# Which tiles of x are turned by DMA, and how k and q of batches 3 to 7 reach their slots

## The chip, the cores and the metric

The kernel runs on one core of one Trainium2 chip. Its time is the device time of one execution in microseconds (us). All figures of the kernel before come from three timed runs and from one execution that was taken with the hardware profiler.

## The reference

The first stage is linear attention with a norm in each head, the second a layer norm, two matmuls with a ReLU between them and a residual:

```python
# q, k, v: (8 batches, 8 heads, 576 rows, 64), float32
kv  = einsum('bhsd,bhse->bhde', k, v)
out = einsum('bhsd,bhde->bhse', q, kv)
out = out / sqrt(mean(out*out, -1) + 1e-6) * g_norm
x   = out.transpose(0, 2, 1, 3).reshape(8, 576, 512)

xn  = (x - mean(x)) / sqrt(var(x) + 1e-6) * g_ln
y   = x + maximum(xn @ w_ch1, 0) @ w_ch2     # w_ch1: 512 x 2048, w_ch2: 2048 x 512
```

## The kernel before, in words

The 8 x 576 = 4608 rows are cut into 36 tiles of 128 rows. A batch has 512 rows in four full tiles, and its last 64 rows share a tile with those of its neighbour: tiles 0 to 3 are batch 0, 4 to 7 batch 1, tile 8 the rests of both; 9 to 12 are batch 2, 13 to 16 batch 3, tile 17 their rests; and so on, so that batches 4, 5, 6 and 7 begin with tiles 18, 22, 27 and 31. Four tiles make a block of the second stage; there are nine blocks. Blocks 0 and 1 do their first matmul tile by tile (`m1_fine`, L582), the others for four tiles at once (`m1_block`, L597, 16 groups of four matmuls of 128x512). The second matmul (`m2`, L616) goes tile by tile in four groups of four. ScalarE evicts each group of the first matmul with a ReLU (L589, L604), VectorE adds the residual to the second (`y_out`, L623), and a DMA from SyncE's queue stores the tile (L629). The matmuls' PSUM tag "mm" has four banks, so TensorE may be at most four groups ahead of the evictions.

Ahead of that lies the work for each batch. GpSimd's queue (POOL) loads k, q and v and turns float32 into bfloat16 on the way. kv is built on TensorE (`kv_mm`, L428) from `kp`, in which k stands in slots of 128 rows with all heads side by side. q stands likewise in `qp`, and one DMA transpose from SyncE's queue (`q_turn_dma`, L420, 128 x 2560 elements) makes `qT` of a whole batch from it. There are three ways for k and q into the slots. Batches 0 and 1 have their own. Batch 2 loads k into `kb` (L232) and q into `qb` (L239) as they lie in memory, 1 KB of four rows at a time, and ScalarE copies them into slot order (L380, two copies for each, 128x1024). Batches 3 to 7 load straight into `kp` and `qp` (`load_slots`, L260, 256 bytes at a time), with no copy. The last 64 rows of each batch come in by a small load of their own (L247).

For each tile the chain is: attention output on TensorE (`t_out`, L451), square on ScalarE (L464), sums and products on VectorE (L473, L468), root on ScalarE (L477), reciprocal, x, its mean (L482 to L520), and xc = (x - mean) * g_ln in bfloat16 (L525). xc must then be turned into `xT`, which the first matmul reads. Tiles 0 to 11 are turned on TensorE (`t_turn_pe`, L532, four transposes) and copied out of PSUM by ScalarE (`t_turn_out`, L539). Tiles 12 to 35 are turned by a DMA transpose from SyncE's queue (`t_turn_dma`, L543).

Nothing is ordered at run time: a planner inside the kernel gives each step a due time and a cost, plays the queues through and writes every engine's instructions down in the order that it finds. An engine works its own list strictly in that order and waits where data are not there. So an instruction that waits holds up everything behind it on its engine. This goes for SyncE too, whose list holds the stores, the turns of q and the turns of x in one row.

GpSimd's loads are held back by "gates": a copy of one element into `mark` (L690) that waits until a certain tile's `xT` is there, for instance tile 11's for k of batch 4, tile 12's for its q, tile 13's for its v. From batch 3 on a second mark (L694, `gate_turn`) holds each k load until the turn of q of the batch before has landed:

```python
            def gate_turn():
                if b >= 3:
                    pool_do(0.1, lambda: nc.gpsimd.tensor_copy(
                        mark, att[b - 1]["qT"][:, 0, 0:1]), [adone[b - 1]["qfree"]])
```

Of the kernel before, what the change touches and what calls it, by code (L numbers as in the profile page):

```python
# [14 lines left out]
def kernel(  # L15
# [11 lines left out]
    nc = tc.nc  # L27
# [6 lines left out]
    B, H, S, D = q.shape  # L34
# [8 lines left out]
    N_TILES = B * S // 128  # L43
    N_BLK = N_TILES // 4
    FINE = (0, 1)
    N_PE_TURN = 12
    N_SUM = 12
    LOOK = 8
    XB = 18
# [129 lines left out]
    def act_cost(n):  # L179
        return n / 1400 + 0.115, n / 1400 + 0.23  # L180
# [33 lines left out]
    kb = [consts.tile([128, H * 6 * D], bf16, name=f"kb{i}") for i in range(2)]  # L214
# [3 lines left out]
    kp = [consts.tile([128, 6, H, D], bf16, name=f"kp{i}") for i in range(2)]  # L218
    qp = [consts.tile([128, 5, H, D], bf16, name=f"qp{i}") for i in range(2)]
    mark = consts.tile([128, 1], bf16, name="mark")  # L220
# [7 lines left out]
    def load_kv(buf, src, b, h0=0, h1=H):  # L228
        t = 6 if b < 2 else 4
        n = 576 if b < 2 else 512  # L230
        def fn():
            nc.gpsimd.dma_start(  # L232
                kv_view(buf, b)[:, h0:h1, :, :].rearrange("p h t d -> p h (t d)"),
                src[b, h0:h1, 0:n, :].rearrange("h (p t) d -> p h (t d)", t=t))
        return fn, n * (h1 - h0) * 256

    def load_q(b, t0, t1):
        def fn():
            nc.gpsimd.dma_start(  # L239
                qb[:, :, t0:t1, :].rearrange("p h t d -> p h (t d)"),  # L240
                q[b, :, 0:512, :].rearrange("h (p t) d -> p h t d", t=4)[:, :, t0:t1, :]
                .rearrange("p h t d -> p h (t d)"))
        return fn, 128 * H * (t1 - t0) * 256
# [7 lines left out]
    def load_slot(dst, src, b, t, h0=0, h1=H):  # L251
# [2 lines left out]
                dst[:, t, h0:h1, :],  # L254
                src[b, h0:h1, 0:512, :].rearrange("h (p t) d -> p t h d", t=4)[:, t, :, :])
        return fn, 128 * (h1 - h0) * 256

    def load_slots(dst, src, b):
        def fn():
            nc.gpsimd.dma_start(  # L260
                dst[:, 0:4, :, :],
                src[b, :, 0:512, :].rearrange("h (p t) d -> p t h d", t=4))
        return fn, 128 * H * 4 * 256


    groups = []
# [24 lines left out]
    att = [dict() for _ in range(B)]  # L291
    done = [dict() for _ in range(N_TILES)]
    adone = [dict() for _ in range(B)]


    rate6, rate4, rate1 = 400.0, 395.0, 305.0
# [24 lines left out]
    def pool_load(name, fnb, rate=425.0, deps=()):  # L321
        fn, nb = fnb
        s = add_dma("POOL", 0, deps, fn, nb, rate)
        load.setdefault(name, []).append(s)
# [339 lines left out]
    def plan_batch(b):  # L664
        p = pos[FIRST[b]]
        ok = okey[FIRST[b]]
        kperm = []
        if b == 1:
            for h0, h1 in ((0, 4), (4, 8)):
                kperm.append(add("ACT", 1.2, 1.35, p - 18, load["k", 1],  # L670
                                 lambda h0=h0, h1=h1: k_permute(nc.scalar, 1, h0, h1)))
            for t in range(5):
                key = (p - 17 + 3 * t) if t < 4 else pos[8] - 40
                if t < 4:
                    qperm = add("ACT", *act_cost(512), key, load["q", 1],
                                lambda t=t: q_permute(nc.scalar, 1, t, t + 1))
                    qread = qperm
                else:
                    qperm = load["q", 1, 4][0]
                add_q_turn_pe(1, t, [qperm, z1[1]], key + 1, ("DVE", "ACT")[t % 2])  # L680
            vdeps = load["v", 1]
            adone[1]["qread"] = qread
            adone[1]["qfree"] = adone[1]["qT", 4][0]
        else:
            f = FIRST[b]
            def gate(n):

                if b >= 3:
                    m, i = divmod(n, 4)
                    pool_do(0.1, lambda: nc.gpsimd.tensor_copy(  # L690
                        mark, blk[m]["xT"][:, 0, i * 128:i * 128 + 1]), done[n]["xT"])
            def gate_turn():
                if b >= 3:
                    pool_do(0.1, lambda: nc.gpsimd.tensor_copy(  # L694
                        mark, att[b - 1]["qT"][:, 0, 0:1]), [adone[b - 1]["qfree"]])
            dk = [adone[b - 2]["kvmm"]]
            if b < 4:

                pool_do(0.5, lambda: nc.gpsimd.memset(kp[b % 2][no_fifth(b), 4, :, :], 0.0), dk)
            gate(f - 7 if b > 3 else 5)  # L700
            gate_turn()
            by_slot = b >= 3
            if by_slot:
                pool_load(("k", b), load_slots(kp[b % 2], k, b), rate1, dk)
            else:
                pool_load(("k", b), load_kv(kb, k, b), rate4, dk)
            pool_load(("k", b), load_fifth(kp[b % 2][:, 4, :, :], k, b), 180.0, dk)
            def some_q():
                gate(f - 6 if b > 3 else 6)
                if by_slot:  # L710
                    pool_load(("q", b), load_slots(qp[b % 2], q, b), rate1, [adone[b - 2]["qfree"]])
                else:
                    pool_load(("q", b), load_q(b, 0, 4), rate4, [adone[b - 1]["qread"]])
                pool_load(("q", b), load_fifth(qp[b % 2][:, 4, :, :], q, b), 180.0,
                          [adone[b - 2]["qfree"]])
            def some_v():
                gate(f - 5 if b > 3 else 7)
                pool_load(("v", b), load_kv(vb, v, b), rate4, dk)
                pool_load(("v", b), load_fifth(v5[b % 2], v, b), 100.0, dk)
            for load_some in (some_v, some_q) if b == 2 else (some_q, some_v):  # L720
                load_some()
            for h0, h1 in ((0, 4), (4, 8))[by_slot * 2:]:
                kperm.append(add("ACT", 0.85, 1.0, ok - 16, load["k", b][0:1] + dk,
                                 lambda h0=h0, h1=h1: k_permute(nc.scalar, b, h0, h1)))
            qperm = []
            for t0, t1 in ((0, 2), (2, 4))[by_slot * 2:]:
                qperm.append(add("ACT", 0.85, 1.0, ok - 14, load["q", b][0:1] + [
                    adone[b - 2]["qfree"]], lambda t0=t0, t1=t1: q_permute(nc.scalar, b, t0, t1)))
            for x in kperm + qperm:
                x.lag = 4.0 if b == 2 else 6.0  # L730
            kperm += load["k", b]
            turn = add_dma("SP", ok - 12, qperm + load["q", b] + (
                adone[b - 3].get("outs", []) if b >= 3 else []),
                           lambda: q_turn_dma(b), 2.6e3, 1.0, occ=2.98, lat=0.25, tail=0.42)
            for t in range(5):
                adone[b]["qT", t] = [turn]
            adone[b]["qfree"] = turn
            turn.lag = 5.0 if by_slot else 0.0
            adone[b]["qread"] = qperm[-1] if qperm else None
            vdeps = load["v", b]  # L740
        outs_before = adone[b - 3].get("outs", []) if b >= 3 else []
        s = add("PE", 1.12 if b > 1 else 1.34, 1.35 if b > 1 else 1.57, (p - 17.5 if b == 1 else ok - 4), vdeps + kperm,
                lambda: kv_mm(b, range(HP)), alloc="kvt")
        a = add("DVE", 0.34, 0.38, (p - 17 if b == 1 else ok - 2), [s, z1[4], z1[5]] + outs_before,
                lambda: kv_out(b, 0, HP, nc.vector, False))
        a2 = add("DVE", 0.34, 0.38, (p - 17 if b == 1 else ok - 2), [a], lambda: kv_out(b, 0, HP, nc.vector, True))
        s.frees = a2
        s.lag = 5.0 if b > 2 else 2.0 if b == 2 else 0.0
        adone[b]["kvmm"] = s
        adone[b]["kv"] = [a2]  # L750


    def plan_tile(n):
        bs, t = TILES[n]
        m, i = divmod(n, 4)
        p = pos[n]
# [38 lines left out]
        for h0, h1 in halves:  # L795
            ff = dict(f0=h0 * D, f1=h1 * D)
            w = (h1 - h0) / H
            xc = add("DVE", 0.6 * w + 0.06, 0.6 * w + 0.15, q0 + 8, [mean, load["gl"][0]],
                     lambda ff=ff: t_xc(n, **ff))
            if n < N_PE_TURN:  # L800
                tp = add("PE", 0.23 * w, 0.23 * w + 0.22, q0 + 9, [xc, ident, m1_before],
                         lambda ff=ff: t_turn_pe(n, **ff), alloc="kvt")
                tp.frees = add("ACT", *cost(act_cost, h0, h1), q0 + 10, [tp],
                               lambda ff=ff: t_turn_out(n, **ff))
                turned.append(tp.frees)
            else:
                turned.append(add_dma("SP", q0 + 9, [xc, m1_before], lambda: t_turn_dma(n),
                              0.5e3, 1.0, occ=1.235, lat=0.25, tail=0.42))
# [145 lines left out]
```

## Time and profile before

| | |
|---|---|
| median of 3 runs | 295.69 us (295.5 to 296.31) |
| the profiled execution's own time | 296.31 us |
| its span in the profile | 294.5 us |
| TensorE busy | 283.4 us, 96% of the span |
| VectorE / ScalarE / GpSimd busy | 165.7 / 143.1 / 66.1 us |
| DMA | 35.21 MB in 106652 packets, of which 85507 under 512 bytes |

The span is the time between the first and the last instruction of the profile; 1.81 us of the execution lie outside it. Engines are named PE (TensorE matmul), PEld (its weight loads), DVE (VectorE), ACT (ScalarE), POOL (GpSimd), SP (SyncE); a q behind the name is that engine's instruction queue. A line such as L597 is the line of the kernel before. "Landing" of a DMA is the time from its issue to its completion.

### The profile page before, as it was taken

The numbers are of one execution on the slowest core, as the hardware profiler recorded it, in microseconds if no ns is written. First come the engines' busy times: TensorE is split into PE (matmuls) and PEld (weight loads), VectorE is DVE, ScalarE is ACT, GpSimd is POOL, SyncE is SP. The second block draws the span as 40 slices with busy tenths as digits, with TensorE's granted clock in tenths as the row PEclk, the third lists the DMA queues.
The fourth block names the chain that finished last, engine by engine and source line by source line (L and its number), as shares of the span: only waits on it lengthen the run. The fifth ranks groups of instructions, "written<-read, shape, count | busy, mean of one in ns | idle before, by whom it ended". The sixth has DMA issues, their size and how long they took to land.

```text
span 294.5 us, 5143 instructions
## 1 busy us (share of the span) xinstructions
PE 283.4 (96%) x2045; PEld 161.2 (55%) x2045; DVE 165.7 (56%) x359; ACT 143.1 (49%) x288; POOL 66.1 (22%) x92
## 2 busy tenths in 40 slices
PE   3989999999999999999999989999999999999994
PEld 1989955977754445444544445444544444444443
DVE  1596048669777877557655764577557755320022
ACT  3278963978847612761276127611761176016400
POOL 8973220208007116120422208020000000000000
PEclk9999999999999999999999999999999999999999
DMA  7999999549989998997399799998201310220012
GB/s 98 186 200 205 204 198 194 162 91 124 185 183 78 120 167 164 175 121 181 64 124 100 94 210 120 123 148 164 56 18 56 89 53 18 67 95 1 0 73 72
DMA packets 106652, 35.21 MB, mean 120 GB/s; under 512 B 85507, under 2 KB 102147, under 8 KB 106628
## 3 DMA queue, kind: packets, MB, share of 16 engines
q0 software_dynamic: 72608, 18.35, 64.8%
q1 hardware_dynamic: 33860, 16.39, 23.5%
q8 instruction: 16, 0.26, 0.4%
q10 hardware_dynamic: 160, 0.13, 0.2%
q14 instruction: 8, 0.07, 0.1%
HBM read 36.70 MB, written 9.44 MB: 157 GB/s over the span
## 4 chain that ended last, share of the span: by engine, by line
PE 87%; DMA 7%; POOL 3%; DVE 1%; issue 1%; ACT 0%; ACTq 0%; POOLq 0%
PE mm_ps L616 39%; PE mm_ps L597 33%; PE mm_ps L582 8%; DMA w<-in_moe_w_ch_dram 5%; PE kv_ps L428 3%; PE out_ps L451 3%; DMA xT<-xc 3%; POOL qp L253 1%; POOL w L333 1%; PE xT_ps L532 1%; POOL kb L232 1%; POOL vb L232 0%; PE qT_ps L400 0%; DVE ss L473 0%; DVE x L503 0%
## 5 line engine op out<-in xcount | busy, mean ns | idle before, releaser
L616 PE MATMUL mm_ps<-w,m 128*128 128x512 bf16 (+1 forms) x592 | 130.2, 373 | 0.0
L597 PE MATMUL mm_ps<-xT,w 128*128 128x512 bf16 x448 | 100.8, 379 | 0.8 <-DMA xT<-xc 0.8
L604 ACT ACTIVATE m<-mm_ps 128x512 bf16<-128x512 f32 x112 | 66.8, 597 | 51.3 <-PE mm_ps L597 50.3
L616 PEld LDWEIGHTS <-m 128*128 128x128 bf16 x592 | 56.7, 98 | 59.8
L597 PEld LDWEIGHTS <-w 128*128 128x128 bf16 x448 | 43.0, 98 | 49.6 <-issue 1.2
L623 DVE SCALAR_TENSOR_TENSOR x<-mm_ps,rstd,x 128x512 f32<-128x512 f32 (+1 forms) x37 | 27.1, 734 | 42.2 <-PE mm_ps L616 42.1
L473 DVE TENSOR_REDUCE ss<-sq 128x8 f32<-128x512 f32 (+1 forms) x37 | 24.8, 670 | 46.2 <-ACT sq L464 46.1
L464 ACT ACTIVATE sq<-out_ps 128x512 f32<-128x512 f32 (+1 forms) x37 | 21.5, 584 | 50.8 <-PE out_ps L451 50.8
L582 PE MATMUL mm_ps<-xT,w 128*128 128x128 bf16 x512 | 30.9, 219 | 0.9 <-ACT xT L539 0.7
L582 PEld LDWEIGHTS <-w 128*128 128x128 bf16 x512 | 29.3, 98 | 1.9 <-issue 0.8
L525 DVE SCALAR_TENSOR_TENSOR xc<-x,mv,gl 128x512 bf16<-128x512 f32 (+1 forms) x37 | 27.1, 737 | 1.3 <-DVE mv L520 0.2
L468 DVE TENSOR_TENSOR xg<-out_ps,gn 128x512 f32<-128x512 f32 (+1 forms) x37 | 24.8, 669 | 0.2
L690 POOL COPY mark<-xT 128x1 bf16<-128x1 bf16 x15 | 5.5, 365 | 80.4 <-DMA xT<-xc 67.7
L589 ACT ACTIVATE m<-mm_ps 128x512 bf16<-128x512 f32 x32 | 18.3, 597 | 3.0 <-PE mm_ps L582 2.3
L503 DVE TENSOR_TENSOR x<-xg,inv 128x512 f32<-128x512 f32 x24 | 16.6, 692 | 0.8
L519 DVE BATCH_NORM_STATS2 stats<-x 128x6 f32<-128x512 f32 x24 | 16.6, 690 | 0.5
L477 ACT ACTIVATE rms<-ss,eps_attn 128x8 f32<-128x8 f32 (+1 forms) x37 | 11.0, 298 | 9.9 <-DVE ss L473 9.9
L451 PEld LDWEIGHTS <-qT 128*128 128x128 bf16 x160 | 11.5, 98 | 7.2 <-DVE kv_pack L443 0.3
L443 DVE CAST kv_pack<-kv_ps 64x256 bf16<-64x256 f32 (+1 forms) x18 | 7.1, 392 | 14.2 <-PE kv_ps L428 14.1
L451 PE MATMUL out_ps<-kv_pack,qT 128*128 128x128 bf16 x160 | 15.0, 220 | 0.1
L428 PE MATMUL kv_ps<-vb,kp 128*128 128x128 bf16 (+1 forms) x144 | 11.8, 234 | 3.0 <-DMA vb<-in_v_dram 3.0
L428 PEld LDWEIGHTS <-kp 128*128 128x128 bf16 (+1 forms) x168 | 11.1, 105 | 4.3 <-DVE kp L382 2.3
(61 smaller groups left out, 172.0 us busy)
## 6 DMA issues: line engine op xcount, KB each, us to landing
out_dram<-x SPq DMA_DIRECT2D x32, 256.0 KB, 2.8
w<-in_moe_w_ch_dram POOLq DMA_DIRECT2D x8, 512.0 KB, 12.6
vb<-in_v_dram POOLq DMA_DIRECT2D x6, 512.0 KB, 9.3
kp<-in_k_dram POOLq DMA_DIRECT2D x5, 512.0 KB, 8.2
qp<-in_q_dram POOLq DMA_DIRECT2D x5, 512.0 KB, 9.9
qb<-in_q_dram POOLq DMA_DIRECT2D x2, 512.0 KB, 15.8
out_dram<-x SPq DMA_DIRECT2D x6, 128.0 KB, 5.5
qp<-in_q_dram POOLq DMA_DIRECT2D x10, 64.0 KB, 8.5
```

The source lines that it names most:

```text
L428: nc.tensor.matmul(ps[:, hp, :], lhsT=kp[b % 2][p, t, 2 * hp:2 * hp + 2, :].rearrange("p h d -> p (h d)"), rhs=(v5[b % 2][:, 2 * hp:2 * hp ...
L451: nc.tensor.matmul(o3[:, hp, :], lhsT=att[b]["qT"][:, 4 * t + hp, :], rhs=kv_pack[b % 3][:, hp, :], start=(i == 0), stop=(i == len(bs) - 1))
L464: nc.scalar.activation(sq[:, h0:h1, :], st[n]["ps", h0][:, h0:h1, :], func=AF.Square)
L468: nc.vector.tensor_mul(xg[:, h0:h1, :], st[n]["ps", h0][:, h0:h1, :], gn.to_broadcast([128, h1 - h0, D]))
L473: nc.vector.tensor_reduce(ss[:, h0:h1, :], st[n]["sq"][:, h0:h1, :], axis=AX.X, op=ALU.add)
L525: nc.vector.scalar_tensor_tensor(xc[:, f0:f1], in0=st[n]["x"][:, f0:f1], scalar=blk[m]["mv"][:, i, 0:1], in1=gl[:, f0:f1], op0=ALU.subtrac ...
L582: nc.tensor.matmul(ps[:, d, :], lhsT=w1[c][:, kk, d * 128:(d + 1) * 128], rhs=blk[m]["xT"][:, kk, i * 128:(i + 1) * 128], start=(kk == 0), ...
L589: nc.scalar.activation(st[n]["m1"][:, c, :, :], st[n]["m1ps", c], func=AF.Relu)
L597: nc.tensor.matmul(ps, lhsT=w1[c][:, kk, d * 128:(d + 1) * 128], rhs=blk[m]["xT"][:, kk, :], start=(kk == 0), stop=(kk == nKm - 1))
L604: nc.scalar.activation(blk[m]["m1", c][:, d, :], blk[m]["m1ps", g], func=AF.Relu)
L616: nc.tensor.matmul(st[n]["m2ps", f0], lhsT=m1_piece(n, c, d), rhs=w2[c][:, d, f0:f1], start=(c == 0 and d == 0), stop=(c == 3 and d == 3))
L623: nc.vector.scalar_tensor_tensor(x[:, f0:f1], in0=st[n]["m2ps", f0], scalar=blk[m]["rstd"][:, i, :], in1=x[:, f0:f1], op0=ALU.mult, op1=AL ...
```

## The change

Two parts. First, the x of tiles 8, 9 and 10 is turned by DMA from SyncE's queue; tiles 0 to 7 and 11 stay on TensorE. Second, batches 3 to 7 go the way of batch 2: k and q are loaded as they lie into `kb` and `qb`, and ScalarE copies them into the slots, two copies of 128x1024 for k and two for q; the wait of a k load for the turn of q of the batch before stays for batch 3 alone. `qb` is one buffer, so a q load now waits for the q copies of the batch before. Together with the second part the planner is told other delays for the turn of q (`lag`), since it now comes behind copies.

```diff
-    N_PE_TURN = 12
+    PE_TURN = (0, 1, 2, 3, 4, 5, 6, 7, 11)
...
-    def load_slots(dst, src, b):
...
             def gate_turn():
-                if b >= 3:
+                if b == 3:
                     pool_do(0.1, lambda: nc.gpsimd.tensor_copy(
-                        mark, att[b - 1]["qT"][:, 0, 0:1]), [adone[b - 1]["qfree"]])
+                        mark, att[2]["qT"][:, 0, 0:1]), [adone[2]["qfree"]])
...
-            by_slot = b >= 3
-            if by_slot:
-                pool_load(("k", b), load_slots(kp[b % 2], k, b), rate1, dk)
-            else:
-                pool_load(("k", b), load_kv(kb, k, b), rate4, dk)
+            pool_load(("k", b), load_kv(kb, k, b), rate4, dk)
...
-                if by_slot:
-                    pool_load(("q", b), load_slots(qp[b % 2], q, b), rate1, [adone[b - 2]["qfree"]])
-                else:
-                    pool_load(("q", b), load_q(b, 0, 4), rate4, [adone[b - 1]["qread"]])
+                pool_load(("q", b), load_q(b, 0, 4), rate4, [adone[b - 1]["qread"]])
...
-            for h0, h1 in ((0, 4), (4, 8))[by_slot * 2:]:
+            for h0, h1 in ((0, 4), (4, 8)):
                 kperm.append(add("ACT", 0.85, 1.0, ok - 16, load["k", b][0:1] + dk,
                                  lambda h0=h0, h1=h1: k_permute(nc.scalar, b, h0, h1)))
             qperm = []
-            for t0, t1 in ((0, 2), (2, 4))[by_slot * 2:]:
+            for t0, t1 in ((0, 2), (2, 4)):
                 qperm.append(add("ACT", 0.85, 1.0, ok - 14, load["q", b][0:1] + [
                     adone[b - 2]["qfree"]], lambda t0=t0, t1=t1: q_permute(nc.scalar, b, t0, t1)))
...
-            turn.lag = 5.0 if by_slot else 0.0
-            adone[b]["qread"] = qperm[-1] if qperm else None
+            adone[b]["qread"] = qperm[-1]
...
-            if n < N_PE_TURN:
+            if n in PE_TURN:
```

What the planner makes of it can be read in the order of the two programs' instructions. On PE only the 12 transposes of tiles 8 to 10 go; every other instruction keeps its place. On SP the turns of tiles 8 and 9 stand behind the store of tile 4, that of tile 10 behind the store of tile 5, then come the store of tile 6 and the turn of q of batch 3; later the turn of tile 19 stands ahead of the turn of q of batch 5, behind which it stood before. On ACT three copies of `xT` go and 20 copies into slots come. On POOL four marks go.

More of the change, by code (lines that the diff above doesn't have):

```diff
@@ L256, in load_slot @@
         return fn, 128 * (h1 - h0) * 256
-    def load_slots(dst, src, b):
[L259 to L263, printed above, removed]
     groups = []
```

## The prediction

> **What bounds the kernel now.** I read the page's busy times and slices first, then a table of stages, then the timeline of one engine after another around the places that the change touches.
>
> ```profile
> PE 283.4 (96%) x2045; PEld 161.2 (55%) x2045; DVE 165.7 (56%) x359; ACT 143.1 (49%) x288; POOL 66.1 (22%) x92
> PEclk9999999999999999999999999999999999999999
> ```
>
> ```profile
> 0.00:25.00 25.00, 18.69 (x231) 16.38 (x232) 14.72 (x44) 12.16 (x29) 19.25 (x33) 1.00 1.25 167
> ...
> 160.00:175.00 15.00, 14.24 (x72) 6.55 (x71) 10.98 (x21) 2.51 (x6) 1.76 (x3) 1.00 1.20 142
> ...
> 265.00:294.50 29.50, 25.42 (x134) 12.86 (x132) 3.22 (x5) 8.47 (x15) 0.00 (x0) 0.98 0.11 37
> ```
>
> The stage table's columns are window, length, then PE, PEld, DVE, ACT, POOL busy, clock, DMA share, GB/s. TensorE is the bound: of the 11.1 us in which PE is idle, 6.3 lie in the first 25 us, 4.1 at the end, and only 0.76 between. The clock is full. So a saving on ACT, DVE, POOL or DMA is worth nothing unless it removes PE work or that 0.76 us; and a new wait of PE is paid in full, since PE has no slack to give it back.
>
> The 0.76 us are here (timeline, three lines):
>
> ```profile
> 163.65 3.38 SPq L420 DMA_TRANSPOSE qT<-qp  x1
> ...
> 167.12 2.19 SPq L543 DMA_TRANSPOSE xT<-xc  x1
> ...
> 174.80 3.40 PE L597 MATMUL mm_ps<-xT,w 128*128 128x512 bf16 x15 [0.76 <-DMA xT<-xc]
> ```
>
> xc of tile 23 is ready at 162.4 (161.68 + 0.75), but its turn stands on SP behind the turn of q of batch 6, which itself waits for q's load (its small load, issued at 155.26, takes 8.2). The turn lands 7.4 us after issue, and block 5 starts late.
>
> **Part one, tiles 8 to 10 turned by DMA.** PE loses 3 x 0.22 us (the chain shows each tile's four transposes of L532 at 0.22): 0.67 us off the path, as PE is busy all through that stretch. ACT loses three copies of 0.58. SP gains three turns of 1.2 us issue. Their xc are done at 68.4, 71.7 and 75.7 (DVE's rows of L525); block 2 starts at 84.52 before, so 83.85 now. Turns of x land in 2.4 to 7.8 us; the worst for tile 10 gives 75.8 + 7.8 = 83.6, just in time. Cost nothing; if tile 10's turn were held on SP by the store of tile 5 (its y is done at 73.9) there would still be 2 us. So -0.67.
>
> The Trainium skill speaks against this part: "VectorE: DVE Perf Modes", section "Rules for kernel authors", says to turn 128x128 on TensorE where PSUM may be the destination, and gives the DMA path 1309 ns against 390 ns. The rows here agree that the DMA takes longer (2.4 us at least against 0.22 + 0.58), but by the rule the change would cost time, and by the rows the longer path is hidden.
>
> **Part two, the loads.** POOL's issue falls from 2.0 us (L260) to 0.9 (L232): nobody on the path waits for it. ACT gains 20 copies; a pair takes 1.99 us (58.26, L380, batch 2), so 4 us a batch. ACT is 49% busy, and beside a block's first matmul an eviction takes 0.60 of 0.86 us, with four banks ahead. Two copies cost PE nothing if k is there when ACT reaches them. Two places are tight. For batch 5 k is let go at 109.75, issued at 110.3, and ACT reaches its copy at 118.25, behind the second eviction. For batch 7: issued at 177.6, reached at 183.8. Loads of this shape (v, L232) land in 6.5 and 7.0 us in quiet, 9.3 to 9.5 in company: k is there at 117 to 120 and at 184 to 187. PE's four banks cover 2 to 3 us of that; I take 0, with an upper end of 1.4 for batch 7 (k at 187, its copy done at 188, the group that wants the bank due at 187.9, and a second copy behind the next eviction).
>
> **The turn of q of batch 3 is where the price lies.** Before:
>
> ```profile
> 82.33 3.23 SPq L420 DMA_TRANSPOSE qT<-qp  x1
> ```
> ```profile
> 83.71 0.19 POOL L690 COPY mark<-xT 128x1 bf16<-128x1 bf16 x1 [9.52 <-ACT xT L539]
> 88.08 0.19 POOL L694 COPY mark<-qT 128x1 bf16<-128x1 bf16 x1 [4.18 <-DMA qT<-qp]
> 88.76 2.02 POOL L260 DMA_DIRECT2D kp<-in_k_dram  x1 [0.49 <-PE kv_ps L428]
> ```
> ```profile
> 84.52 2.75 PE L597 MATMUL mm_ps<-xT,w 128*128 128x512 bf16 x12
> ...
> 89.95 0.39 PE L451 MATMUL out_ps<-kv_pack,qT 128*128 128x128 bf16 x4
> ```
>
> The turn is issued at 82.33 and lands at 87.9; tile 13's output, which reads it first, stands on PE at 89.95: 2 us of slack. The k load of batch 4 was ready to go at 83.71, and POOL held it 4.18 us for the turn. The change does two things to this. First, the turn comes behind ACT's copies. ACT's order is now: root of tile 11 (77.64 before, some 0.2 earlier now), two k copies, a root, a square, a square with sum, two q copies. From start to start that is 77.4 + 0.2 + 1.9 + 0.2 + 0.5 + 0.6 + 1.9 = 82.7, so the copies end, and the turn is issued, at 82.9. Batch 3's loads landed at 74.0 (k), 78.3 and 78.7 (q) before and are issued no later now; ACT reaches the copies at 77.6 and 80.8, so it doesn't wait. Second, tile 11's copy follows (done at 83.4), the mark 0.1 later, and 0.6 after it (as from 101.59 to 102.19) the k load: 84.1, 1.2 us behind the turn and beside it. How long does a turn of q take then? The DMA view gives each turn's landing; these are batches 2, 3, 6 and 7:
>
> ```profile
> qT<-qp SPq DMA_TRANSPOSE x1, 4.9
> ```
> ```profile
> qT<-qp SPq DMA_TRANSPOSE x1, 5.6
> ```
> ```profile
> qT<-qp SPq DMA_TRANSPOSE x1, 10.4
> ```
> ```profile
> qT<-qp SPq DMA_TRANSPOSE x1, 9.6
> ```
>
> Batch 2's had no load beside it; batch 3's met the end of a v load; batch 6's (163.65) met a v load issued at 163.52, batch 7's (190.74) one issued at 191.83. Batch 4's took 6.1, meeting the end of a v load issued 4.3 us before. The bounds are 4.9 and 10.4; the nearest row is batch 7's, with a load of the same shape and size 1.1 us behind it: 9.6. So the turn lands at 82.9 + 9.6 = 92.5, and tile 13's output, due at 89.95 - 0.67 = 89.3, waits 3.2 us. PE works in order, so everything behind it moves. The turns of tile 12's x and the q load gated by it come later too, but have slack until 114.8, the start of block 3.
>
> The Trainium skill says in "Advanced Engine Details and Errata", section "X-Bar Transpose (TRN2)", that such transposes are as fast as regular DMAs, 350 to 400 GB/s; by that the 0.66 MB of a turn would take an estimated 1.9 us, no wait would come and the sum would be 294.3. The trace's shortest is 4.9, and beside loads twice that.
>
> **Later batches.** The k load of batch 5 loses its hold too (112.69 before), but tile 18's output is at 119.9 and the turn of batch 4, now issued at about 107.7 behind its copies, lands by 117.3 even at 9.6. In batches 6 and 7 the turn had landed when the gate opened: nothing moves. For block 5's 0.76 us: q of batch 6 is issued at 153.6 with only a turn of x beside it, 7.0 us, in at 160.6; ACT's copies then run from 160.5 to 162.6, the turn of q goes 1.05 us earlier than before, and tile 23's turn with it: 173.5, under PE's 174.0. Gain 0.7; bounds 0.76 of gain and, if q takes 9.3, a wait 1.25 longer.
>
> **Sum** against the profiled span: 294.5 - 0.67 + 3.2 - 0.7 = 296.3, for that execution 298.1. It lies 0.62 above the median of the three runs, so against the median 295.69 + 1.8 = 297.5.
>
> **Rivals.** What decides is one number, the landing L of batch 3's turn: the change of time is about 82.9 + L - 89.95 - 0.7, which is nothing at 7.75.
> (1) The turn is not slowed: the k load's first packets come late, and the turn is half done. L of 4.9 to 6.1 as in batches 2 and 4; it lands by 89.0 and nothing waits. Then -0.67 - 0.7 = -1.4: 294.3, faster. For it speaks that GpSimd needs 0.9 us to issue; against it batch 7, where this was so as well.
> (2) L of 7 to 8.5: gain and loss cancel, 295.0 to 296.4.
> (3) As forecast, but ACT also waits for a k or q load, in batch 5, 6 or 7: 1.4 to 2 us more, 299 to 299.5; or the ACT list runs 1 us later in batch 3: the same.
>
> **How the numbers follow.** Forecast 0.57, own range 296.9 to 299.0 (L of 9 gives 296.9, L of 10.4 298.3, and 299.0 without block 5's gain); rival 1 0.17, rival 2 0.17, rival 3 0.09. A difference under 0.3% (0.89 us) is about what a measurement of this kernel cannot tell from none; so faster is under 294.8, slower over 296.6. Faster 0.17 (rival 1), same 0.18 (rival 2 and an edge), slower 0.65. The range leaves out rival 1 at its full gain and what rival 3 can add above 300: 294.5 to 300.0.
>
> **What would show it.** Right: a wait of PE of 3 us ahead of L451 near 89, on the DMA of qT; a landing near 9.6 for the turn at 83; the k load of batch 4 at about 84; no wait at block 5's start. Wrong: that landing under 7, a wait at block 2's start for the turns of tiles 8 to 10, or waits of ACT's copies on loads that show as waits of PE behind evictions.

## The result and the profile after

The changed kernel takes 299.39 us (median, 298.86 to 299.58) against 295.95 us of the kernel before in the same comparison (295.5 to 296.31): ratio 1.0114, 95% interval 1.0093 to 1.0135. So it is slower by 3.4 us. The forecast was slower by 1.8, 297.5 us. In a second comparison the same changed kernel gave 299.35 against 296.35, ratio 1.0112 (1.0088 to 1.0137).

The page's first line for the changed kernel, and TensorE's timeline where it waited (its lines named here are 7 lower than those of the kernel before: L590 is the first matmul in blocks, L444 the attention output, L525 the turn on TensorE, L518 xc, L413 the turn of q, L536 the turn of x by DMA, L373 the copies into slots):

```profile
PE 283.2 (95%) x2033; PEld 160.8 (54%) x2033; DVE 165.6 (56%) x359; ACT 158.3 (53%) x305; POOL 54.2 (18%) x88
```
```profile
83.27 0.40 PE L525 MATMUL xT_ps<-identity,xc 128*128 128x128 bf16 x4 [0.28 <-DVE xc L518]
...
86.71 2.75 PE L590 MATMUL mm_ps<-xT,w 128*128 128x512 bf16 x12 [1.32 <-ACT xT L532]
...
94.21 0.40 PE L444 MATMUL out_ps<-kv_pack,qT 128*128 128x128 bf16 x4 [1.91 <-DMA qT<-qp]
...
178.14 4.48 PE L590 MATMUL mm_ps<-xT,w 128*128 128x512 bf16 x20
```

Three waits stand where there was none: two ahead of block 2, one at tile 13's output. The wait at block 5's start is gone (the last line has no bracket). The wait at tile 13 was forecast, the two ahead of block 2 were not. The three are 3.5 us; less the 0.67 us of transposes and the 0.76 us at block 5 that are gone, 2.1 us are lost. The chain of waits between 66 and 96 us tells where they come from:

```profile
69.33 9.75 DMA xT<-xc
...
79.18 0.75 DVE xc L518
...
80.20 0.61 DVE ss L466
...
81.03 1.97 ACT kp L373 x2
83.01 0.20 ACT std L560
83.20 0.48 ACT sq L457
83.69 0.61 ACT junk L542 x2
84.30 1.88 ACT qp L373 x2
86.18 0.07 ACT xT L532
86.25 7.91 DMA qT<-qp
94.16 0.05 issue
94.21 0.40 PE out_ps L444 x4
```

Read from above: the turn of tile 8 by DMA takes 9.75 us to land, and a later xc on VectorE waits for it. VectorE's timeline says by how much; first the same xc before, where it didn't wait, then after:

```profile
74.95 0.75 DVE L525 SCALAR_TENSOR_TENSOR xc<-x,mv,gl 128x512 bf16<-128x512 f32 x1
```
```profile
79.18 0.75 DVE L518 SCALAR_TENSOR_TENSOR xc<-x,mv,gl 128x512 bf16<-128x512 f32 x1 [3.39 <-DMA xT<-xc]
```

That xc is tile 10's. xc has three buffers, and the planner wrote tile 8's xc down ahead of tile 7's, so tile 10 gets the buffer of tile 8, which the DMA still holds. Before, TensorE had turned tiles 8 and 7 by 71.4, and the buffer was free long before tile 10's xc at 74.95. The sums for tile 11 stand behind that xc on VectorE, the root for tile 11 waits for them on ScalarE, and in ScalarE's list the k copies, the q copies and the copy of tile 11's `xT` stand behind that root. So one wait of 3.4 us on VectorE moves block 2's start and the issue of the turn of q alike. The rest is the forecast path: turn of q at 86.25, k load of batch 4 at 87.81 beside it, landing 7.9.

1.0 us of this profile's span belongs to neither. The first kv matmul of the kernel starts at 8.58 us here and at 7.59 before; in the other profiles of this case it starts at 7.07 to 8.33. So it is better to count from the turn of q of batch 2, which lies ahead of all that the change moves: from its issue to the end are 234.2 us before, 236.5 after, and 236.1 in a second profile of the changed kernel. The profiles thus hold 1.9 to 2.3 us of loss, about what the waits come to, and the medians 3.0 to 3.4. Where the rest lies is not known.

### The profile page after: what moved, and what is told of

It reads as the page before. It is cut to its first block, busy times and chain, and to the rows that moved or that the text cites. A ratio compares the mean times of both kernels' runs of the same rounds, so it can differ in the third digit from the quotient of the medians.

```text
span 297.7 us, 5143 instructions
## 1 busy us (share of the span) xinstructions
PE 283.2 (95%) x2033; PEld 160.8 (54%) x2033; DVE 165.6 (56%) x359; ACT 158.3 (53%) x305; POOL 54.2 (18%) x88
## 4 chain that ended last, share of the span: by engine, by line
PE 86%; DMA 8%; ACT 2%; DVE 1%; issue 0%; POOL 0%; DVEq 0%; POOLq 0%
PE mm_ps L609 38%; PE mm_ps L590 31%; PE mm_ps L575 8%; DMA xT<-xc 3%; PE kv_ps L421 3%; PE out_ps L444 3%; DMA qT<-qp 3%; DMA vb<-in_v_dram 2%; PE idle_ps L892 2%; PE qT_ps L393 1%; ACT kp L373 1%; ACT qp L373 1%; PE xT_ps L525 1%; ACT sq L457 0%; ACT m L582 0%
## 5 line engine op out<-in xcount | busy, mean ns | idle before, releaser
L590 PE MATMUL mm_ps<-xT,w 128*128 128x512 bf16 x448 | 100.8, 379 | 1.3 <-ACT xT L532 1.3
L597 ACT ACTIVATE m<-mm_ps 128x512 bf16<-128x512 f32 x112 | 65.9, 597 | 42.9 <-PE mm_ps L590 41.9
L590 PEld LDWEIGHTS <-w 128*128 128x128 bf16 x448 | 43.1, 98 | 50.1 <-issue 1.7
L518 DVE SCALAR_TENSOR_TENSOR xc<-x,mv,gl 128x512 bf16<-128x512 f32 (+1 forms) x37 | 27.1, 737 | 4.5 <-DMA xT<-xc 3.4
L683 POOL COPY mark<-xT 128x1 bf16<-128x1 bf16 x15 | 4.1, 272 | 102.5 <-DMA xT<-xc 85.0
L582 ACT ACTIVATE m<-mm_ps 128x512 bf16<-128x512 f32 x32 | 18.3, 597 | 3.2 <-PE mm_ps L575 2.6
L444 PE MATMUL out_ps<-kv_pack,qT 128*128 128x128 bf16 x160 | 15.0, 220 | 2.0 <-DMA qT<-qp 1.9
L444 PEld LDWEIGHTS <-qT 128*128 128x128 bf16 x160 | 11.5, 98 | 9.3 <-DMA qT<-qp 2.4
L373 ACT COPY kp<-kb 128x1024 bf16<-128x1024 bf16 (+1 forms) x14 | 15.2, 1100 | 0.3 <-DMA kb<-in_k_dram 0.3
```

The source lines that it names most:

```text
L373: eng.copy(o, i)
L444: nc.tensor.matmul(o3[:, hp, :], lhsT=att[b]["qT"][:, 4 * t + hp, :], rhs=kv_pack[b % 3][:, hp, :], start=(i == 0), stop=(i == len(bs) - 1))
L518: nc.vector.scalar_tensor_tensor(xc[:, f0:f1], in0=st[n]["x"][:, f0:f1], scalar=blk[m]["mv"][:, i, 0:1], in1=gl[:, f0:f1], op0=ALU.subtrac ...
L590: nc.tensor.matmul(ps, lhsT=w1[c][:, kk, d * 128:(d + 1) * 128], rhs=blk[m]["xT"][:, kk, :], start=(kk == 0), stop=(kk == nKm - 1))
L597: nc.scalar.activation(blk[m]["m1", c][:, d, :], blk[m]["m1ps", g], func=AF.Relu)
```

## Theories and experiments

Theory A: the loss comes from the turns by DMA, by way of xc's buffer. Theory B, the prediction's: the turns are free and the loads do the harm, by the k load beside the turn of q. In "turns alone" and in the two kernels with batch 3 by slots, lines are those of the kernel before; in the others those of the changed kernel. Each ratio is against runs of the kernel before in the same comparison (medians 296.31, 296.35 and 296.41 us).

| kernel | median us | ratio (95% interval) |
|---|---|---|
| turns alone | 297.38 | 1.003 (1.0011 to 1.0049) |
| loads alone | 299.42 | 1.0102 (1.007 to 1.0133) |
| changed, four xc buffers | 297.67 | 1.0049 (1.0027 to 1.0071) |
| changed, k loads held | 296.83 | 1.002 (1.0003 to 1.0036) |
| changed again | 299.35 | 1.0112 (1.0088 to 1.0137) |
| changed, four xc buffers and hold | 296.04 | 0.9992 (0.9975 to 1.0009) |
| changed, held for batch 4 alone | 297.21 | 1.0024 (1.0008 to 1.0041) |
| changed, held for batch 5 alone | 299.33 | 1.011 (1.0082 to 1.0137) |
| batch 3 by slots, others copied | 295.96 | 0.9985 (0.9972 to 0.9997) |
| the same, 8 and 9 by DMA, four xc buffers | 295.6 | 0.9969 (0.9957 to 0.9982) |
| changed, buffers, hold, 8 and 9 by DMA | 295.3 | 0.9965 (0.9952 to 0.9979) |

### The turns alone

```diff
 # kernel before
-    N_PE_TURN = 12
+    PE_TURN = (0, 1, 2, 3, 4, 5, 6, 7, 11)
...
-            if n < N_PE_TURN:
+            if n in PE_TURN:
```

> The kernel before with tiles 8 to 10 turned by DMA, loads and holds of the k loads as before. Theory A (the turns do the harm: xc has three buffers, so xc of tile 10 must wait until tile 8's turn has landed, and the turns land slowly beside the loads of batch 3): VectorE waits 2 to 4 us ahead of xc of tile 10 near 75 us, block 2 starts 1 to 2 us late; 296.3 to 297.5 us. Theory B (the prediction: the turns are free and save 0.67 us, the loads do the harm): 295.3 us, no wait on a turn of x before block 2.

Measured 297.38 us, ratio 1.003. VectorE's and TensorE's timelines:

```profile
76.76 0.75 DVE L525 SCALAR_TENSOR_TENSOR xc<-x,mv,gl 128x512 bf16<-128x512 f32 x1 [1.37 <-DMA xT<-xc]
```
```profile
85.53 4.48 PE L597 MATMUL mm_ps<-xT,w 128*128 128x512 bf16 x19 [1.00 <-DMA xT<-xc]
```

The wait for the buffer is there with the slot loads too, at 1.4 us. And block 2 waits for tile 10's turn, issued at 77.53, landing 7.9. Block 5's wait stays (0.86). So the turns are not free even alone; theory B's half on them falls. But they cost about a quarter of what the whole change costs, so A is not the whole either.

### The loads alone

```diff
 # changed kernel
-    PE_TURN = (0, 1, 2, 3, 4, 5, 6, 7, 11)
+    PE_TURN = tuple(range(12))
```

> The changed kernel with tiles 0 to 11 all turned on TensorE: the loads' part of the change alone. Theory A: the copies on ScalarE run when planned, the turn of q of batch 3 goes out 3 us earlier than in the changed kernel, at about 83, and what is left is its landing beside the k load of batch 4: 296 to 297 us. Theory B (the loads do the harm): nearly the whole loss of 3.4 us is here, 298.5 to 299.5 us.

Measured 299.42 us, ratio 1.0102: nearly the whole loss, as theory B has it. Here the turn of q goes out at 83.10 (forecast 82.9) and the k load of batch 4 at 84.85; the turn's row in the DMA view, then TensorE's waits, then ScalarE:

```profile
qT<-qp SPq DMA_TRANSPOSE x1, 8.6
```
```profile
91.73 0.40 PE L444 MATMUL out_ps<-kv_pack,qT 128*128 128x128 bf16 x4 [1.49 <-DMA qT<-qp]
...
124.72 6.20 PE L590 MATMUL mm_ps<-xT,w 128*128 128x512 bf16 x27 [1.64 <-ACT m L597]
```
```profile
123.13 1.04 ACT L373 COPY kp<-kb 128x1024 bf16<-128x1024 bf16 x1 [3.09 <-DMA kb<-in_k_dram]
124.08 1.56 ACT L597 ACTIVATE m<-mm_ps 128x512 bf16<-128x512 f32 x3
```

The second wait is the other mechanism that the prediction named and took at 0: ScalarE stands 3.09 us at batch 5's k copy, whose load took 10.3 us, the evictions stand behind it, and TensorE runs out of banks. In the two profiles of the changed kernel ScalarE waits there 0.3 and 0.5 us and TensorE not at all: block 3 starts 2.5 and 1.4 us later there (118.87 and 117.74 against 116.39), and the load took 8.1 and 8.3. That the late block 3 hides this wait is read from the two profiles; it was not tried by itself.

### Four buffers for xc

```diff
 # changed kernel
-        xc = buf(n, "xc", [128, Dm], f0, 3, bf16)
+        xc = buf(n, "xc", [128, Dm], f0, 4, bf16)
```

> The changed kernel with four buffers for xc instead of three; nothing else moves in any engine's order. Theory A: no wait of VectorE ahead of xc of tile 10, root of tile 11 and the copies 2 to 3 us earlier, turn of q of batch 3 at about 84; 1 to 2.2 us faster than the changed kernel, 297.2 to 298.4 us; tile 10's own turn may then be what block 2 waits for. Theory B: the wait for the buffer is hidden, 299.4 us.

Every engine's order is that of the changed kernel; only the buffer differs. Measured 297.67 us, ratio 1.0049 against 1.0112: 0.63% or 1.9 us less. The wait of VectorE is gone, and the turn of q is issued at 83.17:

```profile
84.96 2.53 PE L590 MATMUL mm_ps<-xT,w 128*128 128x512 bf16 x11 [1.00 <-DMA xT<-xc]
...
92.88 0.40 PE L444 MATMUL out_ps<-kv_pack,qT 128*128 128x128 bf16 x4 [2.33 <-DMA qT<-qp]
```
```profile
qT<-qp SPq DMA_TRANSPOSE x1, 9.7
```

So the buffer's wait is worth 1.9 us by the medians, and the two intervals don't overlap. What is left is the prediction's path, with nearly its numbers: 83.17 + 9.7 = 92.87, forecast 82.9 + 9.6 = 92.5. The first line is a second cost of the turns: tile 10's own turn, issued at 75.64, took 9.2 us and held up block 2 by 1.0.

The time of this profile must not be compared: its execution took 299.83 us, 2.2 over the median of its eleven. The page's line of the granted TensorE clock (a digit for each fortieth of the span, 9 for 90% of full speed or more) shows a dip in the slice from 89.4 to 96.9 us:

```profile
PEclk9999999999997999999999999999999999999999
```

In steps of 2 us the clock is 0.97, 0.50 and 0.68 from 92 to 98, just behind the wait at tile 13, and 1.00 on both sides; that is some 1.7 us of work (an estimate from these shares). Of the 33 executions of the kernels that have this wait in their profiles, four have a mean clock of 0.994 (299.83, 300.08, 300.81 and 301.3 us); all other executions here have 0.996 or more. In the profiles of the changed kernel the clock stays full behind the same wait, so whether the wait brings the dip about is not shown.

### The hold back in

```diff
 # changed kernel
-                if b == 3:
+                if b >= 3:
                     pool_do(0.1, lambda: nc.gpsimd.tensor_copy(
-                        mark, att[2]["qT"][:, 0, 0:1]), [adone[2]["qfree"]])
+                        mark, att[b - 1]["qT"][:, 0, 0:1]), [adone[b - 1]["qfree"]])
```

> The changed kernel with the hold back in for all batches: a k load waits for the turn of q of the batch before. Theory A and B alike, if the load slows the turn: the turn of batch 3 lands in about 5 us instead of 7.9, tile 13's output does not wait, 2 us faster than the changed kernel, 297.4 us. Rival C (the turn is slowed by what else is in flight, or is late by itself): landing stays near 7.9 and the time within 0.5 us of the changed kernel.

Measured 296.83 us, ratio 1.002. POOL holds the k load of batch 4 until the turn of batch 3 has landed, and that turn lands in 4.9 us (85.46 to 90.4), before it is wanted; the wait at tile 13 is gone, those ahead of block 2 stay (0.25 and 1.32), and one of 0.38 on a turn of x at 205.67 is new:

```profile
86.34 0.73 POOL L683 COPY mark<-xT 128x1 bf16<-128x1 bf16 x1 [12.28 <-ACT rms L470]
90.45 0.19 POOL L687 COPY mark<-qT 128x1 bf16<-128x1 bf16 x1 [3.38 <-DMA qT<-qp]
90.90 0.89 POOL L232 DMA_DIRECT2D kb<-in_k_dram  x1 [0.27 <-issue]
```
```profile
qT<-qp SPq DMA_TRANSPOSE x1, 4.9
```

Rival C falls: with the turn as late as in the changed kernel and nothing else changed ahead of it, the load alone makes 4.9 into 7.9. The hold recovers 0.92%, 2.7 us, more than the 1.9 us of the wait in the profile. Since the hold also lets the planner move batch 5's k copies further back on ScalarE, there are two more kernels: the hold for batch 4 alone, and for batch 5 alone.

> The changed kernel with the hold back for batch 4 alone (batch 3's was never dropped): the k load beside the turn of q of batch 3 goes, the k load of batch 5 stays free. If the whole gain of e4_hold (1.0112 to 1.002) is the turn of batch 3: the same time as e4_hold, 1.002 to 1.003. If ScalarE's wait for k of batch 5 has a share, as in e2_loads_alone: 1.004 to 1.006.

> The changed kernel with the hold back for batch 5 alone; the planner then writes batch 5's k copies further back on ScalarE, TensorE's and SyncE's orders stay. If batch 5's k has no share in the loss: as the changed kernel, 1.011. If ScalarE's wait for it costs in most executions what it cost in e2_loads_alone's profile, 1.6 us: 1.006 to 1.008.

```diff
 # changed kernel; in the first, then in the second; the mark as in the hold above
-                if b == 3:
+                if b in (3, 4):
...
-                if b == 3:
+                if b in (3, 5):
...
```

Held for batch 4 alone: 297.21 us, ratio 1.0024, within the interval of the full hold. Held for batch 5 alone: 299.33, ratio 1.011 (1.0082 to 1.0137), the changed kernel again. The planner moved batch 5's first k copy back in both, from 122.82 to 125.60 and to 129.47, so it is the second kernel that parts the two: there the copies moved and nothing was gained. So in the changed kernel batch 5's k has no share that these runs can tell (the interval is some 0.8 us to either side), and the gain of the hold is the turn of q of batch 3. Whether the first kernel would keep its gain with the copies where they were was not tried. That turn's landing beside the load was 7.9, 7.6 and 8.1 in three profiles and the wait behind it 1.91, 1.64 and 2.05. Why the timed gain is larger than these waits by 0.6 to 1.1 us stays open.

### Both remedies, and the changed kernel once more

> The changed kernel once more, beside the others on one chip. Theory A+B (wait for the buffer of xc, then the turn of q of batch 3 beside the k load): the same two waits of TensorE, 1.3 to 2 us at block 2 and 1.5 to 2.5 us at tile 13, time 1.0 to 1.2% over before. Whether the first kv matmul of the kernel starts at 8.6 us again (7.6 before) tells if that 0.9 us belongs to the change or to one execution.

The second run of the changed kernel shows the same two places: 1.32 at block 2, 1.64 at tile 13, ratio 1.0112. Its first kv matmul starts at 7.07, not 8.6, so the late start is of one execution.

```diff
 # changed kernel
-                if b == 3:
+                if b >= 3:
...
-        xc = buf(n, "xc", [128, Dm], f0, 3, bf16)
+        xc = buf(n, "xc", [128, Dm], f0, 4, bf16)
```

> The changed kernel with four buffers for xc and with all k loads held for the turn of q. If the two causes together are the loss: no wait at tile 13, about 1 us at block 2 for the turn of tile 10, none at block 5: 0.67 + 0.76 gained against 1.0 lost, 295.4 to 296.2 us, no slower than before. If something else remains: above 297 us.

Measured 296.04 us, ratio 0.9992, the interval includes no change. One wait is left, 0.35 us for tile 10's turn (landing 8.5), in a profile of the fastest of the twelve executions (295.15):

```profile
84.47 2.54 PE L590 MATMUL mm_ps<-xT,w 128*128 128x512 bf16 x11 [0.35 <-DMA xT<-xc]
```

With both waits taken away nothing of the loss remains. The two remedies gain 0.63% and 0.92% alone and 1.2% together. That is less than the sum, as one would expect of waits in one chain, but the intervals are too wide to show it.

### What the copies cost by themselves

```diff
 # kernel before
-            by_slot = b >= 3
+            by_slot = b == 3
```

> The kernel before with batches 4 to 7 going by way of kb, qb and ScalarE's copies, batch 3 straight into the slots, all holds in place, tiles 0 to 11 turned on TensorE: what the copies themselves cost where no turn is late. If copies are free: no wait of TensorE on an eviction, none at block 5, 0.5 to 0.8 us faster than before, 295.2 to 295.7 us. If ScalarE's waits for loads reach TensorE: waits of 1 to 2 us behind evictions in blocks 3 to 5, 297 to 298 us.

Measured 295.96 us, ratio 0.9985 (0.9972 to 0.9997). TensorE has no wait at all after 60 us: the 16 copies are free where their loads are in time, and the wait at block 5 is gone. The gain is 0.4 us where the old wait was 0.76.

> The same as e7_b3_slots, with tiles 8 and 9 alone turned by DMA and four buffers for xc. Both turns land by 81 or 82 us, before block 2 starts at 84: 0.45 us less on TensorE and no wait: 294.8 to 295.3 us. If the turns slow batch 3's loads or the turn of q so far that something waits: 296 us or more.

```diff
 # the kernel just above
-    N_PE_TURN = 12
+    PE_TURN = (0, 1, 2, 3, 4, 5, 6, 7, 10, 11)
...
-            if n < N_PE_TURN:
+            if n in PE_TURN:
...
-        xc = buf(n, "xc", [128, Dm], f0, 3, bf16)
+        xc = buf(n, "xc", [128, Dm], f0, 4, bf16)
```

Measured 295.6 us, ratio 0.9969 (0.9957 to 0.9982), a little above what was expected. No wait of TensorE is left after 60 us. Turned by DMA, tiles 8 and 9 have time to land; tile 10 has not. The same holds for the changed kernel with both remedies:

> e6_xc4_hold with tile 10 back on TensorE, so only 8 and 9 are turned by DMA. TensorE has 0.22 us more, and the wait of 0.35 to 1.0 us for tile 10's turn ahead of block 2 goes: 0.1 to 0.8 us faster than e6_xc4_hold, 295.3 to 295.9 us.

```diff
 # changed kernel with both remedies
-    PE_TURN = (0, 1, 2, 3, 4, 5, 6, 7, 11)
+    PE_TURN = (0, 1, 2, 3, 4, 5, 6, 7, 10, 11)
```

Measured 295.3 us, ratio 0.9965 (0.9952 to 0.9979), no wait of TensorE after 60 us. The last two are faster than the kernel before by 0.3% and than the changed kernel by 1.4%. Their intervals overlap each other and that of 0.9985, where tiles 0 to 11 are all turned on TensorE, so a gain from turning tiles 8 and 9 by DMA is not shown.

## Why the prediction fell short

**Part one, "cost nothing", is the step that failed.** TensorE did lose 0.67 us there: tile 9's output starts 0.92 us later than before, tile 12's 0.24. But the step looked only at when a turn's result is wanted and missed what its source holds: a DMA keeps its xc buffer until it has landed, 9.75 us here, where TensorE was done with two tiles in 0.61. So the xc of tile 10 was done at 79.93 and not at 75.7, the root of tile 11 began at 80.83 and not at 77.4, and the turn of q went out at 86.25 and not at 82.9. The wait for the buffer is worth 1.9 us by the run with four of them. The second half of the step, the worst landing of 7.8, was too low as well: beside the three loads of batch 3 the turn of tile 10 took 7.9 us with the turns alone and 9.2 with four buffers, and block 2 waited for it, which the prediction had named as a sign of being wrong. It took its worst from stretches with fewer loads.

Putting the three turns back on TensorE gains less than the fourth buffer (1.0102 for loads alone against 1.0049), as its profile shows another wait in their place: that of the copies for batch 5.

**The turn of q, the place of the price, was right.** Without the buffer's wait the issue (83.17 for 82.9) and the landing (9.7 for 9.6) came as worked out. That the landing fits so well is in part luck: the forecast put all of it down to the k load of batch 4, but at 83.17 the v load of batch 3 (landed at 86.1) and tile 10's turn (84.8) were still on their way, and with that k load held the turn took 6.0 at the same place. With no turn of x there it took 8.6. The size agrees: with four buffers the kernel takes 297.67 us, about 1.4 us over before, where the forecast of 1.8 was for a kernel without the buffer's wait. In the changed kernel itself the turn went out 3.35 us later than forecast and landed in 7.9, the k load being 1.56 us behind it and not 1.2; so the shorter landing gave back half of the delay.

**The copies on ScalarE.** Taken at 0 in the sum, and 0 in the changed kernel (hold for batch 5 alone: no difference). In the loads alone the same place shows 1.64 us, above the upper end of 1.4 that was given, and for batch 5, not for batch 7: batch 5's k load was issued at 112.83, not 110.3, and took 10.3 us, not 9.5 at the most.

**Block 5's wait** went, as forecast (0.76 to 0). The rivals: the first (the load does not slow the turn) fell to the run with the hold; the second did not come; the third, "the ACT list runs 1 us later in batch 3", had the right place, but it was 3 us, for another cause. Its 299 to 299.5 us hold the measured 299.39 by luck.

**The rule on transposes.** What the Trainium skill says in "VectorE: DVE Perf Modes", section "Rules for kernel authors", TensorE for 128x128 where PSUM may be the destination, is what the turns alone bear out at 1.003 (the two durations that the prediction gives with it stand in the section before it, "The three transpose paths"). Yet tiles 8 and 9 by DMA, with a buffer more, belong to the fastest kernels here; so in these runs the landing and the buffers decide, not the duration of one turn.

## What to carry to other kernels

When work moves from an engine to a DMA, follow its source as well as its result: the buffer stays taken until the DMA has landed, so count the buffers between that step and the next writer, in the order in which the program asks for them. Take a landing time from a stretch with the same traffic beside it, and use the longest such row for whatever must be there in time. On a kernel bound by one engine, an added wait on another engine costs nothing until the chain behind it reaches the bound; look down that engine's list for what stands behind the wait.

## What the runs showed of the hardware

A turn of q (128 x 2560, 0.66 MB) lands in 4.9 to 5.0 us with nothing large beside it (batch 2 in all kernels; batch 3 in the changed kernel with the hold), and in 7.6 to 9.7 with one load of 1 MB of float32 issued 1.1 to 1.8 us behind it. In between lie turns that meet only the end of other transfers: batch 3's took 5.6 before, 6.0 with both remedies and 7.3 with the turns alone.

A turn of x (128 x 512) lands in 2.4 us alone and in 9.75 beside the three loads of batch 3 (k and q issued 2.6 and 0.7 us ahead of it, v 3.9 behind): a fourfold spread for the same instruction. The loads pay as well: batch 3's q load took 9.9 us before and 10.0 in the loads alone, but 11.4 in the changed kernel and 13.3 in the turns alone, where turns of x ran beside it.

Loads of q in 256-byte pieces took 9.5 to 10.4 us before; in 1 KB pieces those of batches 4 to 7 took 6.0 to 6.2, and batch 3's 11.4. Most q loads of the kernel before also started right behind a k load, so the fairest pair is batch 6, where in both kernels k had landed first: 9.5 and 6.0. The size of the pieces was not tried alone. The DMA packets fell from 106652 to 77564.
